# Sorted routing attention beside an FFN: how the sorted pairs bring q and k across, and when their steps are issued

## The chip, the cores and the metric

The kernel runs on one NeuronCore of one Trainium2 chip. The metric is the device time of one execution in microseconds (us), as a median of several runs; lower is better. One further execution was taken by the hardware profiler, and all rows below are from it.

## The reference

For 4 batches of 8 heads with 768 tokens of 64 numbers, every query and key is given to the nearest of 16 centroids of its head (largest dot product of the normalized vectors). A query attends only to the keys of its own cluster; the result of all heads, 3072 rows of 512, goes through a bilinear FFN.

```python
q_assign = np.argmax(np.einsum('bhsd,hcd->bhsc', q_n, c_n), axis=-1)
k_assign = np.argmax(np.einsum('bhsd,hcd->bhsc', k_n, c_n), axis=-1)
mask = q_assign[:, :, :, None] == k_assign[:, :, None, :]
scores = np.where(mask, scale * np.matmul(q, k.transpose(0, 1, 3, 2)), -1000000000.0)
attn = softmax(scores);  x = np.matmul(attn, v)      # then to rows of 512
out = (x @ w_a) * (x @ w_b) @ w_out                  # 512 -> 1536 -> 512
```

## The kernel before

Two heads make a pair; a batch has four pairs, and there are 16. The first four pairs (batch 0) are done "densely": all scores of 768 x 768, with far-off clusters pushed away by a one-hot matmul. The other twelve are "sorted" (`sorted_pair(n, ...)`, n = 0 to 11): the rows of q, k and v are written to DRAM lists by cluster with indirect DMAs, read back in strips, and only blocks on the diagonal are computed.

A sorted pair is a chain of steps:

- `load_blocks` (L1032): eight DMAs read q and k straight from the inputs in blocks of 32 numbers (128-byte runs) into `qks`; `across` (L1042): two VectorE 32x32 transposes make the transposed copy `qkT`.
- `similarities` (L1048): eight TensorE matmuls with the centroids (fp32 matmuls stand twice each in the trace, transposes once). `assign` (L1063): six VectorE steps in a row find the cluster of each row. `prefix` (L1084): seven matmuls count rows before each row. `index` (L1096): seventeen VectorE steps in a row give each row its place in the list.
- `load_rows` (L1151): six DMAs read q, k and v again, by rows of 256 bytes. `put` (L1162): 24 indirect DMAs from GpSimd's queue write them to the lists `qd` and `kvd`, a `kvd` row being k, v, a one and a filler (520 bytes).
- `reload` (L1184): twelve DMAs read the lists back in four strips; `turn` (L1200): four VectorE transposes; `scores` (L1207): 64 small matmuls and two exponentials; `values` (L1228): matmuls with v and its column of ones, then VectorE divides; `keep` (L1263): four DMAs to the list `od`; `get` (L1270): twelve indirect DMAs fetch the rows in token order into a tile `xs`; `x_across` (L1281): six TensorE transposes into `xT`, the FFN's input.
- `clear` (L1008): the lists must hold zeros where no row was put, the column of ones above all. So one or two DMAs of zeros run for every pair, on three sets of lists in turn.

All DMAs except the indirect ones are issued on SyncE's queue (SP), in program order. A DMA whose data or room isn't ready holds every later one there.

The program is written out in an order that a planner finds while the kernel is built. `now[0]` is a planned time; `at(t, f)` puts a step on a heap; `spend(us)` moves `now` on by the planned TensorE time of what was just issued; `run_due()` issues the steps that are due. Each pair has a start (`STARTS`: 17, 64, 136, 192, then every 52 from 244), each step an offset from it, a least gap after the step before it, and a gate. FFN work is a queue of pieces (2.59 us planned for four chunks of 384 columns); while steps wait for their due time, FFN pieces are issued. The dense pairs take 24 groups, 4 us planned each from 14 on. Rounding of the FFN weights (`round_w`, five VectorE steps, one ScalarE, one GpSimd; 512 KB loaded each) runs beside all this: 8 parts in the dense groups, 28 more every 5 us from planned time 106 on. When the puts of pair 1 are issued and the dense pairs are over, `late_room` (L980) gives the dense pairs' memory to the sorted ones; `reload` needs it. TensorE's FFN matmuls all stand on L595 (`in_halves`), and rotate over three PSUM banks which VectorE and ScalarE empty.

FFN output is stored by `store` (L598), whose DMA is issued right behind the VectorE step that makes the data.

Of the kernel before, what the change touches and what calls it, by code (L numbers as in the profile page):

```python
# [10 lines left out]
FP32 = mybir.dt.float32  # L11
# [129 lines left out]
def short_path(nc, tc, ctx, c, cn, centroids_in, casts, n_far, q, k, v,  # L141
# [456 lines left out]
    def store(b, j, half, y):  # L598
        order = "(j p) (half n) -> p j half n" if b > 0 else \
            "(p j) (half n) -> p j half n"  # L600
        rows = out[b * S:(b + 1) * S, :].rearrange(order, j=NJ, half=2)
        nc.sync.dma_start(out=rows[:, j, half, :], in_=y)

    def ffn_block(b, blk):
# [334 lines left out]

    def run_due():  # L940
        while events and events[0][0] <= now[0]:
            t, _, f = heapq.heappop(events)
            f(t)
# [3 lines left out]
    ROWS, KV, BLK = 1280, 2 * D + 2, S // 32  # L947
    kvd = [dram.tile([2 * ROWS + 32, KV], FP32, name=f"kvd{n}") for n in range(3)]
    qd = [dram.tile([2 * ROWS + 32, D], FP32, name=f"qd{n}") for n in range(3)]
    od = [dram.tile([2 * ROWS + 32, D], FP32, name=f"od{n}") for n in range(2)]  # L950
    zrow = zero.tile([P, D + 1], FP32, name="zrow")
    before_mine = zero.tile([P, P], BF16, name="before_mine")
    all_mine = zero.tile([P, P], BF16, name="all_mine")
    oh = zero.tile([P, 2, NJ + 1, 2 * NC], BF16, name="oh_s")
    extra = xtp.tile([P, NCH, S], FP32, name="xT").rearrange("p c s -> p (c s)")
    qk_early = [extra[:, n * 2 * S:(n + 1) * 2 * S] for n in range(2)]
    B_ = {"qks": qk_early[0], "qkT": qk_early[1]}

    def rows_of(t):
        B_["qr"] = t[:, 0:2 * NJ * D].rearrange("p (a j d) -> p a j d", a=2, j=NJ)  # L960
        n = 2 * NJ * (D + KV)
        B_["kvr"] = t[:, 2 * NJ * D:n].rearrange("p (a j d) -> p a j d", a=2, j=NJ)
        nc.gpsimd.memset(B_["kvr"][:, :, :, 2 * D:], 1.0)
        return n

    def sorted_constants():
# [5 lines left out]
        nc.vector.memset(oh, 0.0)  # L972

    def early_room():
        t = hp_.tile([P, NF * HB], FP32, name="h")
        n = rows_of(t)
        B_["simx"], B_["V"] = t[:, n:n + HB], t[:, n + HB:n + 2 * HB]
        B_["cmp"] = t[:, n + 2 * HB:n + 2 * HB + 512]

    def late_room():  # L980
        dense.close()
        post = ctx.enter_context(tc.tile_pool(name="post", bufs=1))
        sizes = (2 * S, 2 * S, 20 * D, 20 * D, 20 * (D + 1))
        big = [post.tile([P, size], FP32, name=f"big{n}")
               for n, size in enumerate(sizes)]
        rows_of(post.tile([P, 2 * NJ * (D + KV)], FP32, name="rows"))
        B_["xs"] = [post.tile([P, NJ, P], FP32, name=f"xs{n}") for n in range(2)]
        temp = post.tile([P, 2 * HB + 512], FP32, name="temp")
        B_["simx"], B_["V"] = temp[:, 0:HB], temp[:, HB:2 * HB]
        B_["cmp"] = temp[:, 2 * HB:]  # L990
        first = lambda i, n: big[i][:, 0:n]
        B_["qks"], B_["qkT"] = big[0], big[1]
        for i, name in ((2, "sq"), (3, "sk"), (0, "sqT"), (2, "skT")):
            B_[name] = first(i, 20 * D)
        B_["P"] = [first(3, 2 * 448), first(1, 2 * 448)]
        B_["O"] = first(0, 20 * D)
        B_["v"] = first(4, 20 * (D + 1))
        is_late.append(True)

    is_late = []  # L1000
    done = set()
# [6 lines left out]
    def clear(n):  # L1008
        if n < 2:
            nc.sync.dma_start(out=od[n][2 * ROWS:], in_=zrow[0:32, 0:D])  # L1010
        if n < 3:
            nc.sync.dma_start(
                out=kvd[n][0:2 * ROWS].rearrange("(p x) d -> p (x d)", p=P).rearrange(
                    "p (x d) -> p x d", d=D + 1),
                in_=zrow[:, None, :].broadcast_to((P, 20 * KV // (D + 1), D + 1)))
            nc.sync.dma_start(  # L1016
                out=qd[n][0:2 * ROWS].rearrange("(p x) d -> p x d", p=P),
                in_=zrow[:, None, 0:D].broadcast_to((P, 20, D)))
        else:
            nc.sync.dma_start(  # L1020
                out=kvd[n % 3][0:2 * ROWS, D:2 * D + 1].rearrange(
                    "(p x) d -> p x d", p=P),
                in_=zrow[:, None, :].broadcast_to((P, 20, D + 1)))
        done.add(("clear", n))

    def sorted_pair(n, start, gather_at):
# [3 lines left out]
        vec = nc.vector  # L1030

        def load_blocks():  # L1032
            qks = B_["qks"].rearrange("p (w j d) -> p w j d", w=2, d=32)
            for w, src in enumerate((q, k)):
                for i in range(4):
                    a, d = divmod(i, 2)
                    nc.sync.dma_start(  # L1037
                        out=qks[32 * i:32 * i + 32, w],
                        in_=src[b, 2 * hp + a, :, 32 * d:32 * d + 32].rearrange(
                            "(x t) d -> t x d", t=32))  # L1040

        def across():  # L1042
            M["qkT"] = B_["qkT"].rearrange("p (w n) -> p w n", w=2)
            for w in range(2):
                vec.transpose(out=M["qkT"][:, w],  # L1045
                              in_=B_["qks"][:, w * S:(w + 1) * S])
# [745 lines left out]
```

## Time and profile before

| | us |
|---|---|
| median of 3 runs (lowest to highest) | 1099.72 (1099.51 to 1102.22) |
| the profiled execution, whole | 1102.22 |
| its span, first to last instruction | 1100.5 |
| VectorE (DVE) busy | 663.3 |
| ScalarE (ACT) busy | 203.5 |
| GpSimd (POOL) busy | 501.1 |
| mean granted TensorE clock | 0.926 of full |

The profile's engines are PE (TensorE matmuls), PEld (its weight loads, which overlap), DVE, ACT, POOL and SP. A row of the waits says "engine line <- who released it: us in total, times, longest". A row of the timeline says "start, duration, engine, line, what"; the bracket at its end is the idle time of that engine just before, and the releaser. A row of groups gives the number of instructions, busy us, and mean ns of one. The lines L1032 to L1295 are the steps of a sorted pair.

### The profile page before, as it was taken

To read this page: it belongs to the slowest core of one execution; us is meant where nothing else is said; L and a number is where in the kernel's file an instruction comes from. 1 tells how busy PE (TensorE), PEld (TensorE's weight loads), DVE (VectorE), ACT (ScalarE), POOL (GpSimd) and SP (SyncE) were. 2 spreads that over 40 slices of the span, in tenths; PEclk is the share of its full clock that TensorE was granted. 3 is DMA by queue.
4 is the path that set the end of the run, shared out by engine and by line. 5 is a ranking of instruction groups with operands and counts; after the bars stand their busy time and mean duration, and the time that the engine had idled before them with its cause. 6 is when DMAs were issued, how large, how long until landed. Compare 5 with 4: busy or idle time off the path is not lost.

```text
span 1100.5 us, 20566 instructions
## 1 busy us (share of the span) xinstructions
PE 945.0 (86%) x8178; PEld 504.4 (46%) x8178; DVE 663.3 (60%) x1516; ACT 203.5 (18%) x434; POOL 501.1 (46%) x487
## 2 busy tenths in 40 slices
PE   7784899754768588987989898978999999999998
PEld 4332344422334255653545464635454566444465
DVE  5854876665474737646584866556675564555662
ACT  4352442211112110101112110102121200112100
POOL 1262651245668767673747474765757300000000
PEclk9896899887888789998999998999999999999999
DMA  9998292889596958789978729596936101000001
GB/s 187 154 129 152 65 129 77 152 173 158 138 190 126 191 95 113 156 109 154 133 113 127 120 67 161 117 149 117 168 82 104 36 24 39 1 1 1 1 25 38
DMA packets 341287, 117.53 MB, mean 107 GB/s; under 512 B 321984, under 2 KB 329664, under 8 KB 341184
## 3 DMA queue, kind: packets, MB, share of 16 engines
q1 hardware_dynamic: 326944, 96.66, 54.9%
q0 software_dynamic: 13824, 19.05, 7.8%
q8 instruction: 67, 1.10, 0.4%
q10 hardware_dynamic: 416, 0.43, 0.1%
q14 instruction: 36, 0.29, 0.1%
HBM read 75.65 MB, written 40.43 MB: 105 GB/s over the span
## 4 chain that ended last, share of the span: by engine, by line
PE 55%; DVE 13%; DMA 12%; SPq 7%; POOL 7%; issue 5%; ACT 0%; DVEq 0%; POOLq 0%; ACTq 0%
PE m L595 45%; DMA big<-kvd 3%; PE s L1215 3%; SPq L1037 3%; POOL kvd L1164 2%; POOL qd L1164 2%; DMA big<-in_k_dram 2%; SPq L1190 2%; PE s L1237 2%; DMA qd<-h,idx 1%; PE s L1246 1%; SPq L1016 1%; DMA big<-qd 1%; DVE big L1204 1%; POOL xs L1271 1%
## 5 line engine op out<-in xcount | busy, mean ns | idle before, releaser
L1271 POOL DMA_INDIRECT xs<-od,idx x144 | 146.7, 1019 | 62.0 <-issue 36.1
L1164 POOL DMA_INDIRECT qd<-rows,idx x120 | 123.7, 1031 | 109.1 <-DVE idx L1146 43.1
L1164 POOL DMA_INDIRECT kvd<-rows,idx x120 | 124.0, 1034 | 35.9 <-issue 32.9
L595 PE MATMUL m<-xT,wa_sb 128*64 128x384 f32 x672 | 124.8, 517 | 3.3 <-DVE h L626 3.3
L595 PE MATMUL m<-xT,wb_sb 128*64 128x384 f32 x672 | 123.0, 509 | 1.3 <-DVE wb_sb L289 1.3
L595 PE MATMUL m<-wo_sb,h 128*64 128x256 f32 x768 | 86.7, 379 | 0.0
L595 PE MATMUL m<-raw 128*64 128x384 f32 x432 | 79.6, 489 | 7.1 <-DVE raw L699 7.1
L1215 PE MATMUL s<-big,big 32*64 32x64 f32 (+1 forms) x1536 | 47.7, 323 | 41.8 <-DVE big L1204 33.6
L734 DVE TENSOR_TENSOR ha<-ha,m 128x384 f32<-128x384 f32 x72 | 39.5, 548 | 73.1 <-PE m L595 52.4
L595 PEld LDWEIGHTS m<-xT,wa_sb 128*64 128x64 f32 x672 | 49.6, 145 | 66.9 <-issue 58.6
L595 PEld LDWEIGHTS m<-xT,wb_sb 128*64 128x64 f32 x672 | 49.0, 143 | 63.9 <-issue 55.8
L734 DVE TENSOR_TENSOR h<-h,m 128x384 f32<-128x384 f32 x72 | 39.5, 550 | 59.9 <-PE m L595 37.1
L731 ACT COPY h<-m 128x384 f32<-128x384 f32 x72 | 34.4, 478 | 212.3 <-PE m L595 212.3
L595 PE MATMUL m<-xT,h 128*64 128x256 f32 x576 | 68.1, 393 | 0.0
L595 PEld LDWEIGHTS m<-wo_sb,h 128*64 128x64 f32 x768 | 55.0, 137 | 28.4 <-issue 1.4
L1215 PEld LDWEIGHTS s<-big,big 32*64 32x64 f32 (+1 forms) x1536 | 41.3, 209 | 53.6 <-DVE big L1204 41.3
L282 POOL TENSOR_TENSOR wa_sb<-wa_sb,rest 128x512 f32<-128x512 f32 x12 | 15.5, 1293 | 89.1 <-DVE rest L277 89.0
L595 PEld LDWEIGHTS m<-xT,h 128*64 128x64 f32 x576 | 42.3, 142 | 23.2 <-issue 4.0
L595 PE MATMUL m<-xT,size 128*64 128x384 f32 x288 | 52.7, 487 | 0.0
L595 PEld LDWEIGHTS m<-raw 128*64 128x64 f32 x432 | 30.9, 137 | 45.7 <-issue 42.6
L1204 DVE STREAM_TRANSPOSE big<-big 128x640 f32<-128x640 f32 x48 | 37.7, 823 | 19.0 <-DMA big<-kvd 11.4
L1052 PE MATMUL O<-big,cTb 128*32 128x192 f32 x160 | 13.2, 422 | 39.4 <-DVE big L1045 39.4
(242 smaller groups left out, 1519.4 us busy)
## 6 DMA issues: line engine op xcount, KB each, us to landing
big<-kvd SPq DMA_DIRECT2D x48, 162.5 KB
big<-qd SPq DMA_DIRECT2D x48, 160.0 KB
big<-kvd SPq DMA_DIRECT2D x48, 160.0 KB
od<-big SPq DMA_DIRECT2D x48, 160.0 KB
raw<-in_moe_w_a_dram SPq DMA_DIRECT2D x12, 512.0 KB
raw<-in_moe_w_b_dram SPq DMA_DIRECT2D x12, 512.0 KB
raw<-in_moe_w_out_dram SPq DMA_DIRECT2D x12, 512.0 KB
kvd<-zrow SPq DMA_DIRECT2D x9, 650.0 KB
```

Of the source, the lines that this page charges most:

```text
L282: nc.gpsimd.tensor_tensor(out=w, in0=w, in1=rest, op=ALU.add)
L595: nc.tensor.matmul(out=ps[half], lhsT=lhsT[:, half], rhs=rhs, **kw)
L731: nc.scalar.copy(out=box[name], in_=box["X"][:, 0:HB])
L734: nc.vector.tensor_tensor(out=box[name], in0=box[name], in1=box[bank][:, 0:HB], op=ALU.add)
L1037: nc.sync.dma_start(out=qks[32 * i:32 * i + 32, w], in_=src[b, 2 * hp + a, :, 32 * d:32 * d + 32].rearrange("(x t) d -> t x d", t=32))
L1052: nc.tensor.matmul(out=ps[32 * kq:32 * kq + 32, w * 192:(w + 1) * 192], lhsT=cTb[:, hp, :], rhs=M["qkT"][:, w].rearrange("p (j k t) -> p k ...
L1164: ins = nc.gpsimd.indirect_dma_start(out=dst[:, :], out_offset=bass.IndirectOffsetOnAxis(ap=M["idx"][:, w, j, a:a + 1], axis=0), in_=src[: ...
L1190: after_puts(nc.sync.dma_start(out=to[32 * s:32 * s + 32], in_=src[strip(s), 0:D].rearrange("(x t) d -> t x d", t=32)), w)
L1204: vec.transpose(out=M[t][:, h], in_=M[s][:, :, 32 * h:32 * h + 32])
L1215: nc.tensor.matmul(out=tiles[s // 2][r0:r0 + m, s % 2, c0:c0 + m], lhsT=M["skT"][r, h, 32 * x:32 * x + m], rhs=M["sqT"][r, h, 32 * x:32 * ...
L1237: nc.tensor.matmul(out=ps[:, s, 65 * i:65 * i + 65], lhsT=pt[:, P * i:P * i + P], rhs=vt[:, i, :], start=True, stop=True)
L1271: nc.gpsimd.indirect_dma_start(out=B_["xs"][n % 2][:, j, a * D:(a + 1) * D], out_offset=None, in_=od[n % 2][:, :], in_offset=bass.Indirect ...
```

## The change

- **q and k.** `load_blocks` and its two VectorE transposes go. `load_rows` now comes first in a pair's chain: eight DMAs of 256-byte rows (q, k twice, v; token = 6 x partition + j), into rooms for two pairs in turn. `across` becomes twelve TensorE transposes of 128 x 128 from these rows, in three steps of four, each copied out of PSUM by ScalarE.
- **Zeros.** The lists are cleared once for each of two sets (n < 2), and no more. A `kvd` row is k and v, 512 bytes. The column of ones is computed: after the puts began, VectorE finds how many keys each place of the list has (`overflow` to `in_order`), and after the reload `filled` writes ones where the place number is below the count and `only_filled` multiplies v by that column.
- **VectorE steps spread.** `assign` is six steps, `index` seven steps and four later ones, `turn` four, `filled` and `only_filled` three; each is a step of the chain with a planned gap of 1.15 us (0.1 for the four that run between the puts), so that FFN work gets in between.
- **Issues spread.** `store` and the load of the next weights are put on the heap 3 us later (and rows go out in the order 6 x partition + j for all batches). `run_due` runs also in the middle of each dense group and after each FFN piece. The second half of batch 0's FFN (`blk == 1`) takes its room only after the puts of pair 1.
- **get** writes into the last chunk of the batch's `xT` in place of `xs`, so it waits in the plan for that room, and for the `x_across` of the pair before.
- **Plan.** `STARTS` becomes 34, 70, 146, 184, then every 51 from 236. Offsets: `load_rows` -31, `across` -23, `similarities` -19, `assign` -17, `prefix` -9, `index` -7, puts 0, `reload` +35, `turn` +41, `scores` +49, `values` +53, `keep` +58. Before: `load_blocks` -20, `across` -12, `similarities` -10, `load_rows` -10, `assign` -9, `prefix` -6, `index` -5, puts 0, `reload` +36, `turn` +41, `scores` +45, `values` +49, `keep` +51.

```diff
     def store(b, j, half, y):
...
-        nc.sync.dma_start(out=rows[:, j, half, :], in_=y)
+        at(now[0] + 3.0,
+           lambda t: nc.sync.dma_start(out=rows[:, j, half, :], in_=y))
...
             if f == 0:
+                while blk == 1 and ("put", 1) not in done:
+                    spend(1.0)
+                    run_due()
                 box["h"] = hp_.tile([P, NF, HB], FP32, name="h")
...
     def clear(n):
...
+        for t, w in ((kvd[n], 2 * D), (qd[n], D)):
             nc.sync.dma_start(
+                out=t[0:2 * ROWS].rearrange("(p x) d -> p x d", p=P),
+                in_=zrow[:, None, 0:w].broadcast_to((P, 20, w)))
...
+        def load_rows():
+            qr, kvr = M["qr"], M["kvr"] = R_["qr"][parity], R_["kvr"][parity]
+            kk = M["kk"] = R_["kk"]
+            for a in range(2):
+                for src, to in ((q, qr[:, :, a]), (k, kk[:, :, a]),
+                                (k, kvr[:, a, :, 0:D]), (v, kvr[:, a, :, D:])):
                     nc.sync.dma_start(
+                        out=to,
+                        in_=src[b, 2 * hp + a].rearrange("(p j) d -> p j d", j=NJ))
+        def across(i):
+            M["qkT"] = R_["qkT"].rearrange("p (w j t) -> p w j t", w=2, j=NJ)
+            ps = side()
+            for x in range(4):
+                w, j = divmod(4 * i + x, NJ)
+                nc.tensor.transpose(
+                    out=ps[:, x * P:(x + 1) * P],
+                    in_=(M["qr"], M["kk"])[w][:, j].rearrange("p a d -> p (a d)"),
+                    identity=ident)
+            nc.scalar.copy(out=R_["qkT"][:, i * 512:(i + 1) * 512], in_=ps)
+            spend(0.5)
...
+            def in_order():
+                M["cnt"] = small.tile([P, E], FP32, name="cnt")
+                vec.tensor_reduce(out=M["cnt"],
+                                  in_=cmp.rearrange("p a c d -> p (a c) d"),
+                                  axis=AX.X, op=ALU.add)
...
+            ], [
+                overflow,
+                lambda: vec.tensor_tensor(
+                    out=cmp, in0=halves(rank_of)[:, :, None, :].broadcast_to(shape),
+                    in1=order_of[:, None, :, None].broadcast_to(shape),
+                    op=ALU.is_equal),
+                lambda: vec.tensor_tensor(
+                    out=cmp, in0=cmp,
+                    in1=halves(keys)[:, :, None, :].broadcast_to(shape), op=ALU.mult),
+                in_order,
+            ]
...
+        def only_filled(g):
+            part = M["v"][:, 2 * g:2 * g + 2]
+            vec.tensor_tensor(out=part[:, :, :, 0:D], in0=part[:, :, :, 0:D],
+                              in1=part[:, :, :, D:D + 1].broadcast_to((P, 2, 5, D)),
+                              op=ALU.mult)
...
+        add(-31, 0, load_rows, lambda: (n < 3 or was("after", n - 1)) and (
+            n == 0 or n == 1 and was("sims", 0) or n > 1 and bool(is_late) and was("put", n - 2)
+            and (n < 3 or was("values", n - 2))))
+        for i in range(3):
+            add(-23, 6 if i == 0 else 1.2, lambda i=i: across(i),
+                (lambda: n == 0 or was("sims", n - 1)) if i == 0 else yes, True)
+        add(-19, 2.5, similarities, lambda: n == 0 or was("after", n - 1), True)
+        row(-17, 2, later("assign", 6))
+        add(-9, 2.5, prefix, hard=True)
+        row(-7, 1.2, later("find", 7))
...
+        add(35, 3.5, reload, lambda: bool(is_late) and (n == 0 or was("values", n - 1)))
+        row(41, 5, [lambda x=x: turn(*x) for x in (
+            ("sq", "sqT", 0), ("sq", "sqT", 1), ("sk", "skT", 0), ("sk", "skT", 1))]
+            + [filled, lambda: only_filled(0), lambda: only_filled(1)],
+            gate=lambda: n == 0 or was("keep", n - 1))
+        add(49, 1.5, scores, hard=True)
+        add(53, 3.5, values, hard=True)
+        add(58, 4, keep, lambda: n < 2 or was("get", n - 2), True)
...
-    STARTS = [17.0, 64.0, 136.0, 192.0] + [244.0 + 52.0 * n for n in range(8)]
+    STARTS = [34.0, 70.0, 146.0, 184.0] + [236.0 + 51.0 * n for n in range(8)]
...
-    for n in range(3):
-        at((8.0, 40.0, 84.0)[n], lambda t, n=n: clear(n))
+    for n in range(2):
+        at((16.0, 50.0)[n], lambda t, n=n: clear(n))
```

More of the change, by code (lines that the diff above doesn't have):

```diff
@@ L1297, in was @@
         def was(*what):
[L1298 to L1301 removed]
+            return what in done
+        last = n == NSORT - 1
         yes = lambda: True
[L1304 to L1314 removed]
@@ L1332, in sorted_pair, with add @@
[L1332 to L1338 removed]
+        chain = []
+        def add(off, gap, f, gate=yes, hard=False):
+            chain.append((off, gap, gate, f, hard))
```

422 lines of the change are left out of this document (209 added, 213 removed).

## The prediction, made before the changed kernel had run

> **What bounds the kernel now.** I read the page's first two parts first.
>
> ```profile
> span 1100.5 us, 20566 instructions
> ...
> PE 945.0 (86%) x8178; PEld 504.4 (46%) x8178; DVE 663.3 (60%) x1516; ACT 203.5 (18%) x434; POOL 501.1 (46%) x487
> ...
> PE   7784899754768588987989898978999999999998
> ...
> PEclk9896899887888789998999998999999999999999
> DMA  9998292889596958789978729596936101000001
> ```
>
> TensorE (PE) is busy 945.0 of 1100.5 us, so 155.5 us of the span it does nothing, and its row of slices shows where: in the first four fifths. There the DMA row is full of nines, and the granted clock falls below 9. In the last fifth PE is at 9 throughout and DMA at 0. A table by stage, with start:end, length and busy time of each engine, then clock and DMA share:
>
> ```profile
> 165.00:350.00 185.00, 134.07 (x1214) 67.64 (x1210) 111.89 (x208) 33.45 (x73) 91.69 (x82) 0.84 0.72 144
> 350.00:850.00 500.00, 438.05 (x4164) 241.67 (x4162) 308.47 (x738) 71.89 (x170) 325.62 (x319) 0.94 0.80 128
> 885.00:1080.00 195.00, 195.00 (x1476) 105.68 (x1476) 107.12 (x276) 23.76 (x53) 0.00 (x0) 1.00 0.05 15
> ```
>
> From 885 on only the last FFN runs, 195.00 of 195.00 us busy at clock 1.00. It can't start before the last sorted pair has ended, and while pairs run, earlier FFN pieces fill PE. So the time is PE's work plus PE's waits, and a wait removed anywhere before 850 comes off the end, unless the queue of pieces runs dry. By the plan it doesn't: 51 or 52 us of every period hold only some 11 us of sorted work, and FFN pieces are left over when the last pair ends.
>
> Next, PE's own waits:
>
> ```profile
> PE O L1052 <- DVE big L1045: 39.4, 12, 8.4
> PE s L1215 <- DVE big L1204: 33.6, 10, 9.2
> PE m L1052 <- DVE xT L1045: 21.5, 4, 15.2
> PE m L535 <- DVE acc L505: 11.7, 3, 6.4
> PE O L1088 <- DVE oh_s L1078: 11.4, 7, 2.7
> PE s L1287 <- DMA xs<-od,idx: 9.9, 2, 9.1
> PE s L1215 <- issue: 7.9, 2, 7.2
> ```
>
> Similarities (L1052) wait 39.4 + 21.5 = 60.9 us, scores (L1215) 33.6 + 7.9 = 41.5, the other three 33.0; together 135.4 of 155.5. VectorE is named, but its transposes wait for DMAs themselves. The longest case, by the timeline:
>
> ```profile
> 65.75 13.87 SPq L1016 DMA_DIRECT2D qd<-zrow  x1
> 79.67 10.94 SPq L1037 DMA_DIRECT2D xT<-in_q_dram  x4
> 93.59 0.98 DVE L1045 STREAM_TRANSPOSE xT<-xT 128x768 f32<-128x768 f32 x1 [17.66 <-DMA xT<-in_q_dram]
> 94.62 0.87 PE L1052 MATMUL m<-xT,cTb 128*32 128x192 f32 x8 [15.23 <-DVE xT L1045]
> ```
>
> One issue of zeros held SP for 13.87 us, the blocks of q behind it took 10.94 us to issue, VectorE sat 17.66 us and PE 15.23.
>
> **What the clock adds.** The same 64 score matmuls, after a wait and without one:
>
> ```profile
> 629.99 4.30 PE L1215 MATMUL s<-big,big 32*128 32x128 f32 x128 [1.67 <-DVE big L1204]
> 851.68 2.46 PE L1215 MATMUL s<-big,big 32*128 32x128 f32 x128
> ```
>
> After a wait of 1.67 us they cost 1.84 us more. Over the whole run:
>
> ```profile
> core 0: 1100.5 us, clock 0.926
> ```
>
> If the clock is either full or half, about (1 - 0.926) / 0.5 = 15% of the span, some 163 us, ran at half rate. [...]
>
> **The change part by part.** Prices of what it adds or removes:
>
> ```profile
> 105.18 1.46 PE m L341 x12
> L349 ACT COPY qkT<-m 128x512 f32<-128x512 f32 x10 | 5.5, 593 | 0.4 <-PE m L341 0.2
> L1045 DVE STREAM_TRANSPOSE big<-big 128x768 f32<-128x768 f32 x20 | 19.2, 971 | 31.5 <-DMA big<-in_q_dram 18.7 <-DMA big<-in_k_dram 12.9
> L1112 DVE TENSOR_TENSOR temp<-temp 128x512 f32<-128x512 f32 x10 | 6.9, 692 | 0.3
> L1116 DVE TENSOR_REDUCE temp<-temp 128x32 f32<-128x512 f32 x10 | 6.9, 686 | 0.3
> L1256 DVE TENSOR_TENSOR big<-s,inv_s 128x640 f32<-128x640 f32 x24 | 19.8, 824 | 9.0 <-ACT dens L1254 9.0
> L1129 DVE TENSOR_SCALAR temp<-temp 128x32 f32<-128x32 int32 x10 | 2.0, 202 | 0.0
> ```
>
> - *Transposes on PE.* The dense pairs do the same twelve in 1.46 us. Twelve pairs: +17.5 us, all on the path, since PE is the bound.
> - *Their copies.* 3 x 0.593 x 12 = 21 us on ScalarE, which is 18% busy: nothing. Without that cover it would be 21.
> - *VectorE.* Per pair 2 x 0.97 go. Two steps like L1112, one like L1116, two like L1256 (each 128 x 640) and four small ones come: 1.38 + 0.69 + 1.65 + 0.81 = 4.5. Net 2.6 x 12 = +31 us. VectorE is 308.47 of 500 busy in the long stage, so FFN steps hide it; where weights are rounded (165 to 350) VectorE gets tight if that stage shrinks. I take +5; bounds 0 and 31.
> - *FFN's second half behind the puts of pair 1.* 24 puts, planned 1.28 us apart, are 31 us; they overlap the end of the dense groups. I take +5; bounds 0 and 10.
>
> What DMAs move, from the page's parts 3 and 6:
>
> ```profile
> q1 hardware_dynamic: 326944, 96.66, 54.9%
> kvd<-zrow SPq DMA_DIRECT2D x9, 650.0 KB
> big<-in_q_dram SPq DMA_DIRECT2D x40, 96.0 KB
> rows<-in_k_dram SPq DMA_DIRECT2D x20, 192.0 KB
> big<-qd SPq DMA_DIRECT2D x48, 160.0 KB
> ```
>
> - *Zeros and loads.* Counted in contiguous runs, a pair loses 2560 of zeros (650 KB by 260 bytes) and 6144 of blocks (eight times 96 KB by 128 bytes), and its row loads grow from six to eight times 768 runs of 256 bytes. Reload (twelve times 640), puts (3072), keep (2560) and get (1536) keep theirs: 28160 runs before, 20992 after, a quarter less. The queue's share, 54.9% of 16 engines over 1100.5 us, is 29.6 ns of one engine per packet, or 1.85 us per 1000 packets on 16. By that a pair takes 52 us of DMA before, as much as its whole planned period, and 39 us after.
> - *Similarities.* `load_rows` gets 8 us planned before `across`, as `load_blocks` had, but no longer shares its stretch with the reload of the pair before (offset +35, thus -16 in the next pair's time) and a second load at -10. The first step needs five of eight DMAs, 3840 runs, 7 us by the price above, and a landing. I leave 2 us per pair, 24 us: 60.9 - 24 = -36.9. Bounds: 0 left, or 45.7 (all but the 15.2 at 94.62).
> - *Scores.* Reload to scores was 9 us planned and becomes 14; `turn` no longer runs as one block behind `index`. I leave 0.5 per pair: 41.5 - 6 = -35.5. Bounds: all left, none left.
> - *Prefix, sums, gathers* (33.0). Spread steps shorten VectorE's bursts; the gathers now wait in the plan. I leave 10: -23. Bounds 0 and -33.
>
> SP's own longest waits on stores:
>
> ```profile
> SPq L602 <- DVE rest L858: 181.7, 10, 114.9
> SPq L602 <- DVE comb L858: 80.7, 18, 10.6
> ```
>
> - *Stores and weight loads 3 us later, two rooms for rows.* A store that waits so holds all DMAs behind it on SP. Most of these waits cost nothing by themselves (114.9 us of them lie in one wait); the loads that they hold up are in the terms of similarities and scores. Behind a `get` that waits for `xT` only puts are queued on GpSimd, at pairs 4 and 8, and GpSimd is 46% busy: 0, or 10 us each if that slack is gone.
> - *Clock.* Twelve pairs with two waits each at 1.84 are 44 us. Waits fall from 135.4 to 40, about 30%, but short ones cost as much as long ones, so I leave 16: -28. Bounds 0 and -44.
>
> **Sum**, on the profiled execution, 1102.2 (span 1100.5 and 1.7 around it): -36.9 - 35.5 - 23 - 28 + 17.5 + 5 + 5 = -95.9, so **1006**. The median of the runs is 1099.7, 0.2% lower, which I neglect.
>
> **The rivals.**
>
> - *Rows still land late.* PE itself now stands at `across` until the DMAs land; the 39.4 us of the late pairs stay, and half of the clock's gain with them: 1102.2 - 21.5 - 35.5 - 23 - 14 + 27.5 = 1036. For it: the lead is still 8 us, and puts run beside it. Against it: a quarter fewer runs and no reload in the same stretch.
> - *Nearly every wait goes.* 1102.2 - 60.9 - 41.5 - 33 - 44 + 17.5 = 940, with some 15 us for VectorE's tight stage and the start, 955.
> - *Slower.* The place is `across`: a transpose waiting at the head of PE's order holds every FFN piece behind it, and SP issues in order, so one held DMA ahead of `load_rows` holds all. Each further microsecond costs 12 us. It decides from 1105.5 - 1006 = 99.5 us, 8.3 per pair, thus from 10.3 us of wait per pair; at 12 us the time is 1126. The row at 94.62 shows that such a wait occurs, 15.23 us, but behind a clear that is gone for late pairs.
> - *It moves waits only.* What PE no longer waits for at L1052 it waits for at the reload, since one DMA system serves both: about 1100. Against it: the DMA need falls to 39 us of 51.
>
> **How the numbers follow.** Forecast 1006 (985 to 1025): 0.52. Late rows, 1025 to 1060: 0.22. Nearly all gone, 940 to 985: 0.15. Slower: 0.07. Waits only moved: 0.04, of which 0.03 within 0.3% (about what a measurement of this kernel can tell from no change) and 0.01 above it. So faster by more than that has 0.89 (the first three), the same 0.03, slower 0.08. The range that leaves out two tenths is 958 to 1055: it cuts about a third of the third case, the end of the second, and both last ones.
>
> **What would show it.** Right: PE's waits in the similarities and scores at some 30 us together, mean clock near 0.97, DMA slices no longer at 9 between 400 and 850, PE's transposes costing 1.5 us a pair, the last FFN starting about 95 us earlier and taking as long. Wrong: waits of over 5 us per pair at the transposes, released by a DMA (rows late); VectorE over 85% busy between 150 and 300 with PE waiting for FFN steps on it (spreading didn't help); FFN pieces used up before the last pair, with PE idle and no releaser near.

## The result and the profile after

The changed kernel is slower: 1175.54 us (median of four runs, 1174.62 to 1179.09) against 1099.62, a ratio of 1.0691 with a 95% interval of 1.0663 to 1.0719. The forecast was 1006, range 958 to 1055. Its profiled execution took 1175.12.

All ratios below are between runs on one chip: on some chips the kernel before took 1092 to 1100 us (the first kind), on three others 1408 to 1415 (the second kind), and only the last section sets times from the two kinds side by side. Rows and periods that are compared come from chips of the first kind, not always from the same one. Two lone executions, 1863.58 us in e3_before_free and 3532.28 us in e7_no_spread_3, are left out of the ratios.

The page of the changed kernel, the same lines as were shown of before:

```profile
span 1173.4 us, 20876 instructions
...
PE 968.3 (83%) x8322; PEld 510.0 (43%) x8322; DVE 684.5 (58%) x1604; ACT 224.0 (19%) x470; POOL 503.0 (43%) x487
...
PE   9988988846782985869969695887959699999998
...
PEclk9988998979796996989979798898979799999999
DMA  9551277663562445325454544355452511000001
...
q1 hardware_dynamic: 234480, 83.80, 33.6%
```

The DMA row is what was forecast: no nine is left between 400 and 850 us (slices 14 to 29 stand at 2 to 5), and the queue's packets fell from 326944 to 234480. It didn't help. TensorE's row has dips at a regular distance up to 930 us, and its clock dips with them. TensorE is busy 23 us longer and idle 1173.4 - 968.3 = 205.1 us instead of 155.5; 23.3 + 49.6 is the 72.9 us by which the span grew. Its own waits say where:

```profile
PE s L1348 <- DMA xT<-od,idx: 148.4, 36, 7.1
PE O L1051 <- DMA rows<-in_q_dram: 19.3, 8, 7.9
...
PE O L1105 <- DVE oh_s L1092: 2.5, 2, 2.1
PE s L1271 <- DVE sq L1242: 2.3, 2, 1.2
```

The waits of the similarities (L1051 now stands for them, 60.9 us before) and of the scores (L1271, 41.5 before) are nearly gone. One wait, `x_across` (L1348) for the gathered rows, went from 9.9 to 148.4 us, 36 times. So the question is why gathers are late. GpSimd's timeline, around the puts (L1204) of one pair and the gathers (L1334) of the pair before it:

```profile
636.62 0.99 POOL L1334 DMA_INDIRECT xT<-od,idx  x1 [5.91 <-PE O L1051]
637.92 0.98 POOL L1204 DMA_INDIRECT kvd<-rows,idx  x1 [0.30 <-issue]
639.20 0.99 POOL L1334 DMA_INDIRECT xT<-od,idx  x1 [0.31 <-issue]
640.49 0.98 POOL L1204 DMA_INDIRECT qd<-rows,idx  x1 [0.30 <-issue]
```

They go in by turns, 1.28 us apart, and ahead of the first gather GpSimd stood for 5.91 us with nine puts of the pair still to come. In the kernel before the twelve gathers stood in a row behind the 24 puts:

```profile
600.05 0.97 POOL L1164 DMA_INDIRECT kvd<-rows,idx  x1 [0.30 <-DMA big<-in_q_dram]
601.33 0.99 POOL L1271 DMA_INDIRECT xs<-od,idx  x1 [0.30 <-issue]
602.62 0.97 POOL L1271 DMA_INDIRECT xs<-od,idx  x1 [0.30 <-issue]
...
615.38 0.96 POOL L1271 DMA_INDIRECT xs<-od,idx  x1 [0.30 <-issue]
```

The place to look is in the diff, at the gate of the first gather. Before it read `(last or ("put", n + 1) in done) and ...`: a pair's gathers were not issued until the puts of the pair behind it were. The changed line has `x_room() and (hp == 0 or was("x", n - 1))`, and that condition is gone.

### The profile page after: what moved, and what is told of

It reads as the page before. It is cut to its first block, busy times and chain, and to the rows that moved or that the text cites. A ratio compares the mean times of both kernels' runs of the same rounds, so it can differ in the third digit from the quotient of the medians.

```text
span 1173.4 us, 20876 instructions
## 1 busy us (share of the span) xinstructions
PE 968.3 (83%) x8322; PEld 510.0 (43%) x8322; DVE 684.5 (58%) x1604; ACT 224.0 (19%) x470; POOL 503.0 (43%) x487
## 4 chain that ended last, share of the span: by engine, by line
PE 42%; POOL 17%; DVE 15%; DMA 11%; issue 10%; SPq 4%; ACT 1%; DVEq 0%; POOLq 0%; ACTq 0%
PE m L595 31%; POOL xT L1334 7%; DMA xT<-od,idx 5%; POOL qd L1204 5%; POOL kvd L1204 4%; PE s L477 2%; DMA od<-sqT 2%; SPq L1042 2%; PE O L516 2%; PE s L1271 1%; DVE acc L505 1%; DMA rows<-in_q_dram 1%; DMA kvd<-rows,idx 1%; PE s L1295 1%; DVE rest L277 1%
## 5 line engine op out<-in xcount | busy, mean ns | idle before, releaser
L1204 POOL DMA_INDIRECT qd<-rows,idx x120 | 125.7, 1047 | 192.2 <-DVE idx L1153 158.6
L1334 POOL DMA_INDIRECT xT<-od,idx x144 | 147.2, 1023 | 91.5 <-issue 36.3
L1348 PE MATMUL s<-ident,xT 128*128 128x128 f32 x72 | 22.1, 361 | 148.4 <-DMA xT<-od,idx 148.4
L1204 POOL DMA_INDIRECT kvd<-rows,idx x120 | 122.8, 1024 | 35.7 <-issue 34.5
L595 PE MATMUL m<-xT,wa_sb 128*64 128x384 f32 x672 | 124.1, 512 | 7.6 <-DVE h L629 7.6
L595 PE MATMUL m<-xT,wb_sb 128*64 128x384 f32 x672 | 122.4, 507 | 0.0
L595 PE MATMUL m<-wo_sb,h 128*64 128x256 f32 x768 | 90.8, 391 | 0.0
L595 PE MATMUL m<-raw 128*64 128x384 f32 x432 | 83.1, 507 | 4.6 <-DVE raw L702 3.0
L1348 PEld LDWEIGHTS s<-ident,xT 128*128 128x128 f32 x72 | 10.1, 158 | 163.0 <-issue 122.3
L595 PEld LDWEIGHTS m<-xT,wa_sb 128*64 128x64 f32 x672 | 48.6, 143 | 69.3 <-issue 57.1
L595 PEld LDWEIGHTS m<-xT,wb_sb 128*64 128x64 f32 x672 | 48.6, 143 | 60.9 <-issue 55.5
L595 PEld LDWEIGHTS m<-wo_sb,h 128*64 128x64 f32 x768 | 55.7, 141 | 30.2 <-issue 4.3
L595 PE MATMUL m<-xT,h 128*64 128x256 f32 x576 | 66.9, 386 | 0.0
L1242 DVE STREAM_TRANSPOSE sqT<-sq 128x640 f32<-128x640 f32 x24 | 19.9, 836 | 58.5 <-DMA sq<-qd 58.4
L595 PE MATMUL m<-xT,size 128*64 128x384 f32 x288 | 52.8, 488 | 1.3 <-DVE h L737 1.3
L595 PEld LDWEIGHTS m<-raw 128*64 128x64 f32 x432 | 31.3, 142 | 44.8 <-issue 38.9
L595 PEld LDWEIGHTS m<-xT,h 128*64 128x64 f32 x576 | 41.2, 139 | 21.7 <-issue 1.7
L282 POOL TENSOR_TENSOR wa_sb<-wa_sb,rest 128x512 f32<-128x512 f32 x12 | 15.6, 1304 | 75.8 <-DVE rest L277 75.7
L734 ACT COPY ha<-m 128x384 f32<-128x384 f32 x54 | 25.9, 479 | 86.8 <-PE m L595 86.8
```

The source lines that it names most:

```text
L282: nc.gpsimd.tensor_tensor(out=w, in0=w, in1=rest, op=ALU.add)
L595: nc.tensor.matmul(out=ps[half], lhsT=lhsT[:, half], rhs=rhs, **kw)
L734: nc.scalar.copy(out=box[name], in_=box["X"][:, 0:HB])
L1204: ins = nc.gpsimd.indirect_dma_start(out=dst[:, :], out_offset=bass.IndirectOffsetOnAxis(ap=M["idx"][:, w, j, a:a + 1], axis=0), in_=src, ...
L1242: vec.transpose(out=M[t][:, h], in_=M[s][:, :, 32 * h:32 * h + 32])
L1334: nc.gpsimd.indirect_dma_start(out=M["xs"][:, j, a * D:(a + 1) * D], out_offset=None, in_=od[parity][:, :], in_offset=bass.IndirectOffsetO ...
```

## The experiments

**Theory.** The dropped gate is the loss. Its rivals at the start: the loss comes from planning `x_across` too close behind its gathers (5 us), which only the alternation exposes; or from some other part of the change.

**e1_gate: the gate put back, all else as changed.**

```diff
-            lambda: x_room() and (hp == 0 or was("x", n - 1)))
+            lambda: (last or was("put", n + 1)) and x_room() and (
+                hp == 0 or was("x", n - 1)))
```

> One gate of the kernel before is put back: the gathers of pair n are issued only after all puts of pair n + 1. Theory A (gathers and puts, issued in the same stretch of the plan, alternate on GpSimd's one queue, so twelve gathers take 25 to 31 us where the plan has 15, and TensorE stands at x_across): a group of twelve gathers takes 14 to 16 us again, the transposes of x_across wait 20 us at most in all where they waited 148, and the time is 1010 to 1040. Theory B (GpSimd's queue as a whole can't keep up with a period of 51 us, whatever the order): the waits turn up at the puts, the reload or the scores, and the time stays above 1130. Theory C (gathers are late because they write into xT, which is still in use): the order doesn't matter, x_across still waits over 100 us, time above 1130.

1051.63 us where the kernel before took 1091.70: 0.9645 (0.9607 to 0.9683). On another chip (e1_gate_2, below) 1051.69 against 1094.28, 0.9611 (0.9561 to 0.9660), with the changed kernel itself at 1174.57 beside it. One condition in the plan is 123 us, and with it the rest of the change is a gain of 3.6 to 3.9%. Theories B and C, which both asked for over 1130, fall. Theory A holds in direction, but its 1010 to 1040 was missed by some 12 us: from the third pair on a group of gathers takes 15 to 17 us again, the first two still take 35 and 27, and `x_across` waits 28.5 us in all, not 20. The page and TensorE's waits of e1_gate:

```profile
span 1044.6 us, 20861 instructions
...
PE 942.2 (90%) x8322; PEld 502.1 (48%) x8322; DVE 683.2 (65%) x1604; ACT 225.1 (22%) x470; POOL 502.5 (48%) x487
...
PEclk9989998996979999999999999999999999999999
```

```profile
PE O L1051 <- DMA rows<-in_q_dram: 23.8, 8, 7.9
PE s L1348 <- DMA xT<-od,idx: 20.3, 4, 6.5
PE O L1105 <- DVE oh_s L1092: 15.7, 7, 4.8
```

The clock row shows the second part of the loss: with 148.4 us of short waits TensorE ran 350 to 930 us at a mean clock of 0.88, without them at 9 from the thirteenth slice on (0.99 from 350 to 850 us, below). TensorE's busy time went from 968.3 to 942.2 with the same 8322 matmuls.

**e2_late_x: gate left out, `x_across` planned 20 instead of 5 us behind the last gather.**

```diff
-        add(0, 5, x_across, hard=True)
+        add(0, 20, x_across, hard=True)
```

> The changed kernel with x_across planned 20 us after the last gather and not 5; the order on GpSimd is left as it is. Theory A: gathers and puts go on alternating (25 to 31 us a group), but FFN pieces fill the time, so x_across waits 25 us at most and the time is 1010 to 1045. Theory B: GpSimd is the bound, so what is gained at x_across is lost at later steps; above 1130. Theory C: the gathers start late by a wait on xT; with 15 us more most of that is hidden too, but groups of gathers begin with a wait of 5 us and more on GpSimd.

1153.61 us, ratio 1.0575 (1.0539 to 1.0611). Theory A's 1010 to 1045 is missed; the time is the one that Theory B asked for, though e1_gate, with the same instructions on GpSimd, rules out B's reason that its queue can't keep up whatever the order. If the wait at L1348 were itself the loss, this would have taken it away. It did take the wait away, and nearly all of the time stayed (some 1175 us with the wait, on other chips). TensorE's waits of e2_late_x:

```profile
PE O L1105 <- DVE oh_s L1092: 56.6, 5, 18.0
PE m L595 <- DVE ha L737: 41.1, 6, 10.7
PE O L1051 <- DMA rows<-in_q_dram: 23.8, 9, 7.7
PE m L595 <- DVE h L737: 17.4, 2, 8.7
...
PE s L1348 <- ACT sk L1282: 4.2, 4, 1.1
```

The idle time reappears at the prefix and inside the FFN. So L1348 was where a delay was seen, not where it is made, and the theory needed a loop that TensorE's waits only follow. One turn of it in the changed kernel, by SP, VectorE and GpSimd in order of time:

```profile
658.61 1.97 SPq L1230 DMA_DIRECT2D sq<-qd  x4
```

```profile
665.15 0.84 DVE L1242 STREAM_TRANSPOSE sqT<-sq 128x640 f32<-128x640 f32 x1 [12.04 <-DMA sq<-qd]
...
674.24 0.83 DVE L1242 STREAM_TRANSPOSE sq<-sk 128x640 f32<-128x640 f32 x1
...
679.96 0.18 DVE L1153 TENSOR_SCALAR idx<-temp 128x24 int32<-128x24 f32 x1
```

```profile
656.32 0.97 POOL L1204 DMA_INDIRECT qd<-rows,idx  x1 [0.30 <-DMA kvd<-rows,idx]
...
658.89 0.97 POOL L1204 DMA_INDIRECT kvd<-rows,idx  x1 [0.30 <-issue]
...
680.42 1.31 POOL L1204 DMA_INDIRECT qd<-rows,idx  x1 [16.73 <-DVE idx L1153]
```

The last put of q of one pair ends at 657.3; 658.61 the reload goes out; VectorE stands 12.04 us for it, since `turn` (L1242) of this pair comes in its order ahead of the list places of the next; those are done at 680.1 (L1153); 680.42 the next pair's first put. The pair's period is thus the length of its puts on GpSimd plus this tail. GpSimd, 43% busy over the span, has no slack inside this loop: a gather in among the puts makes the loop longer, one behind the puts lies in the tail, when GpSimd waits anyway. The mean over the last six passes (first put of the sixth pair to first put of the twelfth, by the rows below; a pair's puts run from its first to the end of its 24th, 12th in the halved kernel, the tail from there to the next first put):

| kernel | puts | tail | period |
|---|---|---|---|
| before | 31.5 | 27.5 | 59.0 |
| changed | 47.0 | 20.2 | 67.2 |
| e1_gate | 31.6 | 24.0 | 55.6 |
| e2_late_x | 46.1 | 20.6 | 66.7 |
| e4_half_puts_3 | 36.8 | 22.6 | 59.4 |
| e7_no_spread_3 | 30.9 | 27.6 | 58.4 |

The first puts of the sixth and the twelfth pair, for the changed kernel and for e1_gate:

```profile
480.71 1.03 POOL L1204 DMA_INDIRECT qd<-rows,idx  x1 [29.47 <-DVE idx L1153]
...
883.91 1.31 POOL L1204 DMA_INDIRECT qd<-rows,idx  x1 [13.72 <-DVE idx L1153]
```

```profile
433.38 1.06 POOL L1204 DMA_INDIRECT qd<-rows,idx  x1 [6.12 <-DVE idx L1153]
...
767.05 1.32 POOL L1204 DMA_INDIRECT qd<-rows,idx  x1 [7.03 <-DVE idx L1153]
```

403.20 / 6 = 67.2 and 333.67 / 6 = 55.6. A pair's puts take 47.0 us where e1_gate has 31.6, 15.4 more. Over these six pairs 9.7 of the twelve gathers start among the next pair's puts in the mean, 12.4 us at 1.28 each, and 2.6 us more GpSimd stands before a gather that isn't ready, with puts behind it. Between the third and the twelfth pair's first put the changed kernel needs 654.8 us (229.15 to 883.91), e1_gate 536.9 (230.11 to 767.05): the difference is 118 of the 128.8 us between these two spans. On one chip (after_again and e1_gate_2) the periods are 67.0 and 56.1, and this stretch makes 111 of 121.8 us. e2's period of 66.7 says why it gained so little.

**e3_before_free: the kernel before, its gate taken out.**

```diff
-                          (lambda: (last or ("put", n + 1) in done) and (
-                              n < 2 or ("x", n - 2) in done)) if i == 0 else yes,
+                          (lambda: n < 2 or ("x", n - 2) in done) if i == 0 else yes,
```

> The kernel before, without its gate that holds the gathers until the puts of the next pair are issued; nothing else. By the plan the two then overlap by only a few steps. Theory A: groups of gathers of pairs 4 to 10 grow from 14 to 16 us to 18 or more, x_across waits 20 to 60 us where it waited 9.9, and the time is 1105 to 1140. Theory B and C: nothing changes, 1097 to 1104, since the count of instructions on GpSimd and the place that the gathers write to are as before.

1107.36 us, ratio 1.0143 (1.0088 to 1.0198). Its wait at `x_across`:

```profile
PE s L1287 <- DMA xs<-od,idx: 23.6, 5, 9.7
```

The time lies in the 1105 to 1140 that Theory A asked for, at its low end, and the wait in its 20 to 60. But the groups of gathers of the later pairs, which were to grow, didn't: only the puts of the third and fourth pair grew, from 55.9 and 49.3 to 68.1 and 65.6 us, with gathers among them. From the fourth group on the gathers stayed in a row at 15 us, since in the old plan they come due only after the next pair's puts. So the gate did little in the kernel before; it became necessary with the new plan, in which both come due together.

**e4: the changed kernel without the puts of the second head** (12 of 24; that head's output is not the reference's). The gathers still go in by turns. It tells whether GpSimd's sum in the loop costs, or only the order of a gather behind a put.

```diff
+            if a == 1:
+                return
```

> The changed kernel with the puts of each pair's second head left out, 12 of 24 (that head's rows of the lists stay as they were, so this part of the output is not the reference's); the plan is as it was and the gathers still go in among the puts. Loop theory (each pair waits for the one before it through puts on GpSimd, reload, turn on VectorE, list places of the next pair, its puts; the twelve gathers in among the puts make the loop some 15 us longer): 12 x 1.28 = 15 us go out of each of nine passes, the time between one pair's x_across and the next falls from 68.6 to some 53 us, and the run takes 1040 to 1075 us. Rival, the order alone (a gather waits behind a put whatever the sum of both is): groups of gathers of 25 us and over as before, x_across still waits 7 us at each of its first transposes, and the time stays above 1130 us. Second rival, a free GpSimd (46% busy, not in any loop): 1165 to 1180.

> The same kernel as e4_half_puts (the puts of the second head left out, so that this part of the output is not the reference's), once more: on the chip of that run the kernel before took 1415 us instead of 1099.6, and TensorE stood 80 us for nothing that the profile names, which is under 2 us on the other chips. Where the kernel before takes about 1095: loop theory 1040 to 1075 us, groups of gathers 19 to 22 us, period of x_across 53 us. Rival, the order of gather behind put alone: x_across waits over 100 us in all, the time stays above 1130.

These two fell on chips of the second kind, where they gave 1201.86 and 1204.61 us without a base. So a third was run with two bases on its chip, the changed kernel and e1_gate.

> The changed kernel as it is, as the base for the other runs on its chip: on two chips the kernel before took 1408 to 1415 us, and what ran there has only the kernel before beside it. Where the kernel before takes about 1095: 1170 to 1180. Where it takes 1400 and over: the loop (GpSimd, reload, VectorE) is longer there too, 1420 to 1520.

> e1_gate again, as the second base. Where the kernel before takes about 1095: 1045 to 1058. Where it takes 1400 and over: GpSimd's order theory says that it beats the changed kernel by 80 us and over there too, 1330 to 1400.

> The changed kernel with the puts of the second head left out (that part of the output is not the reference's), beside its base. Loop theory: the time between one pair's x_across and the next falls by up to 15 us from the base's, 100 to 135 us off the changed kernel's time. Rival, the order of gather behind put alone: less than 45 us off. Where the kernel before takes 1400 and over: 1202 again, and the base tells which.

The bases gave 1174.57 us (1.0736, 1.0683 to 1.0789) and 1051.69, where the kernel before took 1094.28.

1077.14 us, ratio 0.9837 (0.9782 to 0.9892), 97.4 below the changed kernel: just short of the 100 that the loop theory asked for, over twice what the order alone allowed. But the period was 59.4, not 53, and `x_across` still waits:

```profile
PE s L1350 <- DMA xT<-od,idx: 71.4, 26, 6.6
```

Twelve puts of 1.28 us are 15.4; the stretch of puts and gathers shortened only by 10.2, from 47.0 to 36.8. The rest went to a wait on GpSimd itself, ahead of the first gather of a group:

```profile
644.35 0.98 POOL L1336 DMA_INDIRECT xT<-od,idx  x1 [16.03 <-DMA od<-sqT]
```

The gather reads the list `od`, which `keep` writes, and until that has landed it holds the puts behind it: some 10 us a pair here, where it was 2.6 in the changed kernel. At other gathers the row names TensorE instead; whether they waited for the room in `xT` the rows don't settle. So the sum in the loop is the larger part and the order another: a gather that isn't ready stands ahead of puts that are, and half the wait at `x_across` is left.

**e7: e1_gate with the vector steps issued in blocks again** (planned gap 0 instead of 1.15 us).

```diff
-        def row(off, gap, fs, between=1.15, gate=yes):
+        def row(off, gap, fs, between=0.0, gate=yes):
```

> e1_gate with one more part of the change undone: the vector steps of a row are issued one behind the other in the plan, with no 1.15 us between them, so that a pair's list places stand in VectorE's order in one block. The plan is shorter by it (the last x_across at 683 instead of 709). Loop theory: the next pair's list places come some 10 us earlier in VectorE's order, the waits for them on GpSimd (5 to 11 us a pair in e1_gate) shrink, and the time falls to 1025 to 1045. Rival, the spreading does what it is for (VectorE serves the FFN's sums on time): TensorE's waits for VectorE, some 35 us in e1_gate, grow to 60 and more, and the run takes 1060 to 1085.

> The same kernel as e7_no_spread, once more for the same reason (there its ratio to the kernel before was 0.989, e6_apart's 0.960, on one chip). Loop theory: VectorE's block of list places comes some 10 us earlier, 1025 to 1045. Rival, the spreading serves TensorE: TensorE's waits for VectorE over 60 us in all instead of some 35, and 1060 to 1085; the ratio there speaks for the rival.

> e1_gate without the 1.15 us between vector steps, beside e1_gate. Loop theory (VectorE's order decides, the block of places comes earlier): 5 to 25 us below e1_gate. Rival (spreading serves TensorE): 10 to 35 us above it. Where the kernel before takes 1400 and over: 1401 again, and the base tells which.

The first two were on chips of the second kind (below). The third, on the chip of e1_gate_2: 1094.25 us, ratio 0.9993 (0.9968 to 1.0018), 42.6 above e1_gate. The rival, that spreading serves TensorE, holds and is larger than it asked: TensorE's waits for VectorE add up to 69.5 us against 38.8 in e1_gate_2. TensorE's waits of e7_no_spread_3:

```profile
PE s L1348 <- DMA xT<-od,idx: 36.1, 8, 6.3
PE O L1105 <- DVE oh_s L1092: 18.6, 6, 4.5
PE s L1271 <- DVE sq L1242: 10.3, 3, 7.2
PE m L535 <- DVE acc L505: 8.1, 3, 4.8
PE m L595 <- DVE h L737: 8.1, 3, 6.6
```

All rows of waits together are 130 us against 99 in e1_gate_2, the mean clock 0.939 against 0.961. Without the spreading, all the rest of the change, gate included, is worth nothing that can be measured. Nor does a block of places in VectorE's order shorten the tail: it is 27.6 us, 24.6 in e1_gate_2. What the tail waits for first this run doesn't show.

**e5, e6, e8: on chips of the second kind only.** Each was meant to find the last tens of us. e5 issues `turn` of a pair behind the places of the next (gate `last or was("found", n + 1)`); e6 is e1_gate with a pair's puts held back in the plan while gathers are under way; e8 is e1_gate with the prefix planned 5 instead of 2.5 us behind the last assign step.

> The changed kernel with one wait in the plan: the turn of a pair (n of 2 and over) is issued only when the list places of the pair behind it are found. The order on GpSimd is as it was. The plan itself gets longer by some 30 us of planned idle, since nothing fills the time. Loop theory: VectorE no longer stands in the turn, waiting for the reload, ahead of the next pair's list places, so GpSimd gets its places earlier and its waits for them (170.7 us in the changed kernel) fall below 80; with the 30 us taken off again the run takes 1080 to 1120. Rival, GpSimd's order alone is the cause and VectorE's order is nothing: the gathers still stand among the puts, and the time is that of the changed kernel or longer by the planned idle, 1165 to 1210.

> The same kernel as e5_turn_late, once more for the same reason. There the longer plan had by itself drawn most gathers out from among the puts (groups of 14 to 18 us), so it now tests the two causes together, against the gate of e1_gate (1051.6). Loop theory: with both the turn behind the places and the gathers in a row, what is left over e1_gate is the plan's idle time of 30 us: 1070 to 1110. Rival, GpSimd's order is not what decides: 1165 to 1210.

> The same kernel as e5_turn_late, under the same condition: turn of a pair behind the list places of the next one in VectorE's order. The gathers go in nearly a row by themselves (groups of 14 to 18 us from the third pair on), and the plan is 50 us longer than the changed kernel's at the last x_across. Loop theory: waits at x_across under 50 instead of 148 us, 1070 to 1110. If VectorE's order and GpSimd's are no cause: 1165 and over.

> The gate that was dropped is put back (gathers of a pair wait in the plan for the puts of the next, as in e1_gate, 1051.6) and the puts of a pair don't start in the plan while gathers are under way, so that the first two pairs, whose groups of gathers still took 34 and 26 us in e1_gate, have theirs in a row too. All groups at 14 to 16 us. Loop theory: the first groups cost e1_gate up to 20 + 11 us, part of it beside other work, but the plan idles some 10 us a pass for it: 1035 to 1060. If the first groups lay on the path in full, 1020 to 1030; if the planned idle does (90 us), 1100 and over.

> The same kernel as e6_apart, once more for the same reason. There all groups of gathers but the first two took 14 us, and the first two 25 and 26. Against e1_gate (1051.6, groups of 34 and 26 us, then 14 to 16): the first group 9 us shorter, the plan 10 us of idle a pass longer. 1045 to 1075 if half of the planned idle is on the path, 1100 and over if all is, under 1045 if none is.

> The same kernel as e6_apart, on a chip on which the kernel before should take about 1095 us: e1_gate with the puts of a pair held back in the plan while gathers are under way. In e1_gate x_across still waits 28.5 us, 20.3 of it for gathers of the first pairs, whose groups take 35 and 25 us. Here these take 25 or less and x_across should wait under 15; the plan is 10 us longer. 1035 to 1050 if the first pairs' gathers are what is left, 1055 to 1075 if the plan's length is what counts.

> e1_gate with the sums over the list (the prefix) put 5 us instead of 2.5 behind the last assign step in the plan, so that TensorE doesn't stand before it (17.4 us in 7 waits in e1_gate). The waits there go to under 4 us. If TensorE's waits alone count, 1035 to 1045; if the places come 2.5 us later in each of ten pairs and the loop counts them, 1055 to 1080.

Ratios to the kernel before on the same chip: e5 0.9492, 0.9534 and 0.9509 (intervals within 0.9428 to 0.9563); e6 0.9596, 0.9695 and 0.9653 (0.9540 to 0.9751); e8 0.9685 (0.9639 to 0.9731); e7 there 0.9891 and 0.9948 (0.9826 to 0.9971). None of the expected times can be judged, as neither the changed kernel nor e1_gate has a run there. What can be read is that e6 and e8 lie clearly below e7 there, as e1_gate does elsewhere, and that e5 is the lowest of the four; it changes VectorE's and GpSimd's order together, so which of them does it stays open. The best version with a time on a chip of the first kind is e1_gate.

## Why the prediction failed, step by step

- **The step that failed** is in the term "prefix, sums, gathers": "the gathers now wait in the plan. I leave 10: -23." They did wait, for other things. The condition that had kept them behind the next pair's puts was removed in the same line of the diff, and the working read what the new gate adds, not what it drops. The three waits went from 33.0 to 157.6 us (148.4 at the gathers), where no gain at all was the worst bound. e1_gate shows the price of the condition: 123 us.
- **The cover that was named wasn't there.** "GpSimd is 46% busy: 0, or 10 us each if that slack is gone." The share is a mean over the span; in the pass that sets the period GpSimd is a link of the chain (47.0 of 67.2 us puts and gathers), and its free time lies nearly all in the tail. The working did ask what stands behind a `get` that waits, and answered "only puts", but priced it for the room in `xT` alone, at pairs 4 and 8. It didn't price the twelve gathers themselves among the 24 puts, which most of them meet from the third pair on, nor a gather that waits for `keep` ahead of puts.
- **Similarities**, 60.9 to 24 left: measured 20.5 in the changed kernel, 28.7 in e1_gate. Right. **Scores**, 41.5 to 6 left: 4.0 and 4.6. Right, and e7 shows that the spreading is a part of it (14.3 without).
- **DMA.** A quarter fewer runs was forecast; the packets fell by 28%. Right, but it doesn't carry the time: e7 has all of it, with the work that the change adds, and takes the time of before. What it is worth by itself no run tells.
- **Transposes**, 1.46 us a pair: 12.1 + 10.4 + 4.3 us for the three groups at L1051, 2.2 a pair. Off by 9 us, small here. VectorE's tight stage, 5: TensorE's waits for it in the FFN (L595) are 11.9 us after 11.7, so nothing. The other 5, for the FFN's second half, no run isolates.
- **Clock**, -28. The mean clock fell to 0.908 from 0.926. TensorE's busy time grew by 23.3 us, of which 26.8 are the transposes, so its other work took only 3.5 us less. In e1_gate the clock is 0.966, close to the 0.97 that was to show the forecast right, and the other work took 30 us less (busy 942.2 after 945.0, with 27.1 us of transposes): there the term came out. The stage from 350 to 850 us in the changed kernel and in e1_gate (columns as in the prediction's table by stage):

```profile
350.00:850.00 500.00, 385.21 (x3689) 210.50 (x3687) 266.89 (x672) 69.52 (x160) 263.20 (x259) 0.88 0.44 89
```

```profile
350.00:850.00 500.00, 460.74 (x4670) 259.29 (x4672) 337.24 (x845) 87.72 (x202) 324.21 (x318) 0.99 0.55 106
```

  In e1_gate TensorE still stands for 39 us of this stage and keeps a clock of 0.99. By their means the longer waits go with the lower clock: the changed kernel's 36 waits for gathers average 4.1 us (148.4 / 36) and its stage stands at 0.88, while two groups of e1_gate's average 3.0 and 2.2 us (23.8 in 8, 15.7 in 7) and its stage stands at 0.99. Single waits of e1_gate don't sort by length. Two of them, and the clock (the third number from the end) right behind each:

```profile
452.86 0.63 PE L1051 MATMUL O<-ident,rows 128*128 128x128 f32 x4 [2.12 <-DMA rows<-in_q_dram]
...
454.00:458.00 4.00, 4.00 (x16) 1.61 (x14) 1.51 (x4) 1.23 (x3) 3.08 (x4) 0.57 0.20 58
```

```profile
507.12 0.66 PE L1051 MATMUL O<-ident,rows 128*128 128x128 f32 x4 [3.03 <-DMA rows<-in_q_dram]
...
507.00:512.00 5.00, 4.88 (x30) 2.43 (x32) 2.15 (x6) 1.72 (x4) 3.78 (x5) 1.00 1.04 240
```

  So behind a wait of 2.12 us the clock stood at 0.57, as it fell behind the 1.67 us of the prediction's row (0.50 from 632 to 634 us of the kernel before, 1.00 from 626 to 628), and behind one of 3.03 us it stood at 1.00. In the kernel before it stood at 0.61 in the 4 us behind a wait of 2.12 us (807.29) and at 1.00 behind one of 3.66 us (731.38). What the row could not give is a general price: 39 us of waits at a clock of 0.99 cost some 5 us of the 500 by an estimate (500 x 0.01), and 1.84 us for every short wait was too much.
- **What the forecast was of.** e1_gate is the change as the working had understood it, and it gained 40 and 43 us on its two chips where 96 were forecast. The busy time is near the sum (942.2 after 945.0, where -28 and +17.5 make 934.5). The waits are what is missing: the three groups that the sum named, 135.4 us, were to fall to 40 and are 85.5. Similarities (28.7) and scores (4.6) are as forecast; the excess stands in the same term again, `x_across` 28.5, prefix 15.7 and sums 8.0 us where 10 had been left for all three. Of `x_across`, 20.3 us lie at the first two pairs, whose groups of gathers are long: eight gathers of the first (35 us) stand among the third pair's puts, and the second (27 us) among GpSimd's rounding of FFN weights (L282), one of whose steps kept it 6.01 us waiting for VectorE. Why the prefix still waits no run shows; e8, meant for it, has no base.
- **The slower rival** had a chance of 0.07 and the wrong place: `across`, by rows that land late. That wait is 20.5 us in all, 1.7 a pair. "Waits of over 5 us per pair at the transposes, released by a DMA" did appear, 12.4 a pair, at the other transposes.

## What to carry to other kernels

When a gate is rewritten, list the conditions that the old one had and ask of each what runs free without it; an order that nobody needs in the old plan can be the one that holds the new plan together. An engine's free share counts for a moved instruction only at the place where it lands: find the loop that sets the period, and see whether the engine is in it there. And when a planned delay makes one wait vanish and the time stays, the wait was a symptom: measure the period of the loop instead.

## What the hardware showed besides

On three chips the kernels took far longer (the kernel before 1408 to 1415 us), though the main DMA queue's packets did not: in e7_no_spread they took 29.4% of 1396.9 us there, 410.7, and 37.5% of 1089.4, 408.5, on a chip of the first kind. The same kernel in the middle of eight pairs' groups of puts, summed, on a chip of the second kind and then on one of the first (length, then busy time of each engine):

```profile
sum 219.00, PE 109.96 PEld 62.26 DVE 24.23 ACT 9.64 POOL 166.94; mean PE 13.75 PEld 7.78 DVE 3.03 ACT 1.20 POOL 20.87
```

```profile
sum 222.00, PE 215.34 PEld 119.01 DVE 112.28 ACT 39.73 POOL 169.92; mean PE 26.92 PEld 14.88 DVE 14.04 ACT 4.97 POOL 21.24
```

While GpSimd writes rows at the same pace (busy 166.94 of 219 and 169.92 of 222 us), TensorE is busy half of the time instead of nearly all of it, VectorE a ninth instead of half. TensorE's timeline on the chip of the second kind, during one such group:

```profile
666.54 0.35 PE L1304 MATMUL s<-v_s,rows 64*64 64x65 f32 x4 [0.86 <-issue]
668.00 0.48 PE L1304 MATMUL s<-v_s,rows 64*64 64x65 f32 x4 [1.11 <-issue]
669.42 0.48 PE L1304 MATMUL s<-v_s,rows 64*64 64x65 f32 x4 [0.94 <-issue]
```

Matmuls come four at a time, 1.4 us apart, with nothing to wait for that the profile shows. With half the puts left out the loss on such a chip is 127 us (e4, 1204 against 1077), with all of them some 307 (e7, 1401 against 1094). The two kernels differ in the gate and the spreading too, so that the loss goes with the indirect writes is suggested by this and by the stretches above, not shown. What holds the engines there no run tells.
